# A fused attention-and-mixer kernel on one core: two token-weight blocks transposed on TensorE, cos and sin products joined, and the engine orders written anew

## The chip, the cores and the metric

The kernel runs on one core of a Trainium2 chip, in one launch. The metric is the device time in microseconds of that core; the kernel before takes 236.05 us, the median of 3 runs from 234.23 to 237.71. The profiled run took 235.77 us, of which the profile's span covers 233.9.

The engines are named as in the profile: PE is TensorE's matmul stream and PEld its weight loads, DVE is VectorE, ACT is ScalarE, POOL is GpSimd, and SP is the engine whose queue issues every DMA of this kernel.

## The reference

An attention stage feeds a mixer stage. There are 4 batches, 8 heads, 768 positions, head width 64; the mixer's width is 8 x 64 = 512.

```
# attention, per head; chunks of 32 keys, each query keeps 6 of 24
ub     = sum_d max(q * k_min(chunk), q * k_max(chunk))     # a bound for each query and chunk
sel    = the 6 chunks of highest ub that are not in the future
scores = q k^T / 8, masked to sel and to j <= i
attn   = softmax(scores);  x = attn v                      # heads side by side: x is (768, 512)

# mixer, per batch
theta  = x @ w_theta
y      = w_tok_r @ (x * cos(theta)) + w_tok_i @ (x * sin(theta))    # w_tok_* are 768 x 768
u      = x + y
out    = u + relu(u @ w_ch)
```

## The kernel before

**How it is written.** `record()` calls `op()` or `alt()` once for each piece of work: a name, an engine (with `alt`, a choice of engines), a planned duration in nanoseconds, what is read and written, and the function that emits the instructions. The n-th call is number n. The string `ORDER` (L17) then lists these numbers in the order in which they are emitted; a trailing `b` or `c` takes the second or third engine of an `alt`, and `F5` puts 5 small filler matmuls on PE. Each engine runs its own instructions strictly in this order, so `ORDER` fixes five queues. It also hands out buffers: `decode()` gives the next free one of a class at first use and takes it back after the last. The classes and their counts stand in `CLASSES` (L105 on): six landing buffers `ld` for everything that is loaded, three PSUM banks `mi` for most matmul results, two PSUM pairs `sc` for scores, one `av` for attention times v.

**Names used here**, with b for batch, p for a pair of heads, h for a head, t for one of six blocks of 128 positions:

- `Lq`, `Lk`, `Lv` load a pair's q, k, v (one transfer for each head of q and k). `Tq`, `Tk` transpose them on PE in two halves (three 128x128 fp32 transposes each). `evk`, `evq` evict the result from PSUM, `red0`, `red1` take the chunk maxima and minima on DVE, `kd` their difference, `cq` and `relu` derive the two forms of q.
- `ub.b.p` (L482) computes the bounds of two pairs on PE, 32 matmuls. Then a chain on DVE selects the chunks: `t1` (transpose), `cz`, `mx` (nine MAX8), `lt`, `t2`, twice; `cp` copies the masks into `qx`.
- `sc.b.h.s` (L554) are the scores, in three steps for a head, `ex` the exponentials on ACT (L560), `tri` the triangular mask, `av.b.h.i` (L401) the product with v, `norm` the division on DVE. Batch 0 uses a variant of these (L336 to L376).
- The mixer, `mixer(b)`: `Tx` and `evx` transpose x for batches 0 and 1 (batches 2 and 3 do it by DMA, `Dx`). `th.b.t` (L608) is theta, four matmuls of 512 columns; `sin` and `cos` follow on ACT (L615, L619), then the two products `zi = x*sin` and `zr = x*cos` (L623), one instruction each, on DVE or POOL. `mix.b.t.si` (L633, L635) are two 512-column matmuls; block t of y needs all six si. `u` adds x on DVE, `Tu` or `Du` transposes u, `ch` is the product with w_ch, `ot` the last sum on DVE, `out` the store.
- The weights: `Lwth`, `Lwch` and `Lwtok.ri.tt` load, `cwth`, `cwch`, `cwtok` cast to fp16. A token-weight block (ri 0 is real, 1 is imaginary, tt is one of six) must also be transposed: `Twtok.ri.tt` (L702) does this by a DMA from SP's queue. `mix.b.t` reads blocks (0, t) and (1, t).

The pieces of the code that the change touches most are the product and the token-weight transposes:

```
for nm, dst, src in (("zi", zi[t], sn), ("zr", zr[t], cs)):          # L624
    al = [("POOL", 1100, 1, ...), ("DVE", 342, 1, ...)]
    alt(f"{nm}.{b}.{t}", al if nm == "zi" else al[::-1], ...)
...
op("SP", f"Twtok.{ri}.{tt}", 1270, [(a, 0)], [("wtok", (ri, tt))], tr, dma=1200)   # L703
```

Of the kernel before, what the change touches and what calls it, by code (L numbers as in the profile page):

```python
# [10 lines left out]
FP32 = mybir.dt.float32  # L11
FP16 = mybir.dt.float16
ALU = mybir.AluOpType
# [5 lines left out]
    "3 1 4 31 2 29 28 30 0 21 58 17 57 14 18 729 15b F5 5 9 20b 55 730 7 16 10 56 477 11 F19 32 406 36 6 19 "  # L19
    "109 39 44 451 41 8 13b 34 48 12 23 37 75 45 38 42 33 47b 24 22b 40b 450 25 F12 50 35 83 26 68 27 71 51 82 "  # L20
    "69 176 72b 85 161 177 52 162 167 178 84 63 74 59 53 168 405 64 110 164 102 61 163 173 165 65 169 60 174 "
    "54 F9 170 67b 166b 113 77 43c 66 62b 46 171 175 196 78 49b 76 202 79 179 203 185 115 183 197 181 172b 193 "
    "125 80 204 81 90 194 198 190 92 184 91 191 195 199 186 95 200 192 187 96b 98 70b 73 93b 201 86 188 376 "
    "99b 213 103 140 87 211 375 101b 180 88 114 225 401 214 182 94b 210 402 116 104 377 89 189 134 226 126 378 "
    "209 105 228 127 227 216 212 229 205 230 217 222 106 403 207 215b 265 223 404 107 386 218 108 219 266b 389 "
    "224 381 387b 379 100 206 220 111 390 97 412 208 254 413 221 242 382 415 232 255 383b 243 231 256 248 384 "
    "135 233 388b 414 239 249 244 234 131 235 236 136 385 237 240 245 250 238 267 246 391 251 416 241 268 269 "
    "252 380 476 407 247 392 410 128 270b 259 253 411 258 257 393 112c 263 262 141b 260 137 261 394 408 264 "
    "142 395 417 409 132c 271 396b 418 397 133 272 420 419 129c 283 398b 130 421 138c 278 285 424 422 273 139 "
    "423 293 279 287 155 274 427 281b 121 295 146 276b 152 294 297 149 280 428 288 158 296b 275 437 298 429 "  # L30
# [12 lines left out]
    "503 775 747c 504b 507 583 757b 506c 505c 1067 774 601 776 785 598 584 602 820 777 613 786 778 821 593 603 "
    "599 569 787 591 592 570 610b 572 788 594 600 811 573 803 571b 595 779 807 812 798 575 596 574b 1069 780 "
    "822 1070 801 783c 805 606 789 597 576 614 802 784c 604 615 605 792c 826 887 577 607 800 890 616 824 817 "
    "806 823 579 580 799 578 825 793c 804 840 617 581 808b 619 891 781c 618 827 620 625 888 1092 892 906 626 "
    "1091 627 828 889 1071 628 907 893 1072b 629 829 1073b 894 1074 900 631 830 895 897 903 841 1075 898 831 "
    "896 639 1089 899 832b 630 634 633 641 632b 908b 640 644 643 635 642b 649 636 637b 646 638 654 645 648 651 "
    "666 647b 667 656 653b 668 655 669 1090b 657b 659 658 660 650 1135 661 790b 1134 652b 901 687 688 689 662 "
    "690 691 904 902 692 663 782b 905 693 791b 664 670 705 665 867 864 868 911 671 701 865 869b 880 672 909 "  # L50
    "910 881 809 866 702 912 835 810 882 833 836 877 815 834 813c 1113 861 878 839 719 1156 838 862 842 720 "
    "879 814 721 707 852 863 843 837 872 853 874 708 871 854 875 680 709 1114 870 1084 844 873 673 876 1180 "
    "1085 674 845 884 675 855 846 1076 856 681 1077 1159 847 858c 885 857b 1158 883 1078b 850c 682 851b 1079 "
    "1157 929 1080 945 930 683 848c 886 1093 1081b 684 1094 849c 946 685 931 926 859c 686 932 947 927 1095 "
    "860c 704 1100 1098 676 1102 928 1099 958 933 677 1101b 1137 1096 678 1103 1136 934 1097 919 1104 937 959 "
    "935 679 936 1105b 920 1082 960 938 1108 703 1083 1106 921 1109 916 1088 1087b 1086 955 1161 716 1107 1160 "
    "956 1112 710 1111 717 917 913 957 718 711 1110 1115 914 712 918 713 1116 915 1125 924 1117 923 1126 1118 "
    "922 1143 1181 942 1127 1145 939 1144 1119 694 943 1128 695 1120 696 1129 940 1122c 1146 952 1123c 697 925 "
    "1124c 1131b 698 953 941 1147 1130c 1227 714 1133c 699 1228 954 1233 715 700 1138 1121c 1151 1234 944b "
    "1230 706 1132 1141 1229 1152 949 1235 1231 1139b 1240 962 1142 1162 1241 1232 1246 1166 963 1148b 961 "  # L60
    "1164b 950 1247 1242 1243 964 1140 948 1248 1214 1244 951 1149 1173 1163b 1150 1236 968 1245 1220 1174b "
    "1215 1153 1237 1165 1238 1167 1239 1221 967 1154 1175 1204 1176 1169b 1222 1251 1250 1205 1171 1177 965 "
    "1207 1170 1249 722 1216 1208 1252 1172b 1206 970 1168 1217 1209 723 1201 1218 1179 986 724 1155 966 1178c "
    "1202 1182 1219 987 1203 969 1223 1192 1224 1225 1183 971 1226 988 996 989b 972 1184 990 1212 973 1185 "
    "1211 1210 998 981 974b 1186 997 1213 975b 976 982 1187 983 991 999b 978 1189 1188 985 1008 977 980 1256 "
    "992 1000 1253 979b 993 1022 994b 984b 1254 1009 995 1023 1193 1191c 1194 1015 1190c 1016 1195 1017 1196 "
    "1257 1024 1255 1018 1197c 1259 1199c 1010 1200c 1260 1011 1258 1012 1261 1013 1198 1279 1014 1025 1280 "
    "1026 1044 1262 1298 1281 1292 1299 1019 1293 1263 1300 1295 1264 1001 1296 1294 1265 1285 1027 1286 1297 "
    "1282 1028 1020 1287 1283 1269 1046 1021 1303 1301 1270 1302 1284 1266 1304 1045 1289 1267 1271 1272 1290 "
    "1288 1052 1273 1291 1268 1002 1274 1053 1276 1275 1277 1054 1029 1278 1030 1031 1305 1032 1055 1310 1003 "  # L70
    "1056 1004 1005 1309 1006 1036 1007 1037 1306 1038 1311 1307 1033 1312 1034 1039 1308 1035 1040 1041 1313 "
    "1314b 1331 1047 1042 1336 1315 1332 1057 1333 1043 1334b 1058 1337 1335 1316 1338 1339b 1048 1059 1326 "
    "1318 1340 1060 1317 1061 1320 1327 1319 1321 1328 1062 1329b 1376 1063 1322 1330 1362 1323 1324b 1363 "
    "1377 1325 1064 1378 1065 1379 1364 1066 1348 1349 1365 1350 1351 1352 1353 1380 1354 1366 1367 1384 1341 "
    "1368 1342 1343 1386 1049 1344 1050 1345 1346 1051 1355 1347 1356 1357 1383 1394 1358 1395 1359 1360 1396 "
    "1400 1361 1381 1385 1401 1369 1382 1370 1371 1402 1391 1372 1392 1373 1374 1393 1389 1375 1397 1390b 1387 "
    "1398 1406 1388b 1399 1403 1407 1408 1404 1405 "
)

B, H, S, D = 4, 8, 768, 64  # L80
P = 128
DM = H * D
NT = S // P
CH = 32
NCH = S // CH
QS = 192
NS = S - QS
# [3 lines left out]
NEG = -1000.0  # L91
KX = D + NCH
ROW = (0,)
X_DMA = (2, 3)
U_DMA = {(b, t) for b in (1, 2, 3) for t in range(NT) if b < 3 or t < 4}
SEGS = [(0, 4), (1, 3), (2, 5)]
BASE = [0, 1024, 2048]
# [61 lines left out]
def record(G):  # L159
# [417 lines left out]
    def mixer(b):  # L577
# [25 lines left out]
        for t in range(NT):  # L603
# [10 lines left out]
            def sin(ps=ps, sn=sn):  # L614
                nc.scalar.activation(out=T(sn), in_=T(ps), func=AF.Sin, bias=0.0, scale=1.0)  # L615
# [280 lines left out]
```

The softmax here doesn't subtract the row's maximum and nothing guards it: scores larger than these inputs give would overflow.

## Time and profile before

| stretch of the span | what runs in it | what the profile has there |
|---|---|---|
| 0 to 52 us | batch 0's attention, first weights, batch 1's first half | first `th` at 44.27, first `mix` at 51.67 |
| 52 to 88.3 us | batch 0's mixer, batch 1's first four heads | `ub.1.2` (batch 1's second half) starts at about 88.3 |
| 88.3 to 112.7 us | batch 1's last four heads, parts of batch 2 | `th.1.0` starts at 112.69 |
| 112.7 to 233.9 us | mixers of batches 1 to 3, the attention of 2 and 3 | last `ch` ends at 230.15 |

PE runs 2091 matmuls, DVE 517 instructions, ACT 248, POOL 196. The granted PE clock is full nearly throughout (mean 0.997). SP issues 170 DMAs: 64 loads of q and k, 16 of v, 20 of weights, 6 of small constants, 24 stores, and 40 transposes (12 `Twtok`, 12 `Dx`, 16 `Du`).

A reader of such a page should keep apart how long one matmul is shown (a 512-column one has a mean of 379 ns) and how often one can start: in the chain of waits four of them take 0.86 us, 0.216 us each, since they overlap. "Busy" on PE is therefore no measure of how much room is left.

### The profile page before, as it was taken

The numbers are of one execution on the slowest core, as the hardware profiler recorded it, in microseconds if no ns is written. First come the engines' busy times: TensorE is split into PE (matmuls) and PEld (weight loads), VectorE is DVE, ScalarE is ACT, GpSimd is POOL, SyncE is SP. The second block draws the span as 40 slices with busy tenths as digits, with TensorE's granted clock in tenths as the row PEclk, the third lists the DMA queues.
The fourth block names the chain that finished last, engine by engine and source line by source line (L and its number), as shares of the span: only waits on it lengthen the run. The fifth ranks groups of instructions, "written<-read, shape, count | busy, mean of one in ns | idle before, by whom it ended". The sixth has DMA issues, their size and how long they took to land.

```text
span 233.9 us, 5656 instructions
## 1 busy us (share of the span) xinstructions
PE 217.7 (93%) x2091; PEld 125.2 (53%) x2091; DVE 171.0 (73%) x517; ACT 165.2 (71%) x248; POOL 98.0 (42%) x196
## 2 busy tenths in 40 slices
PE   6999999898899997788999999999999999999993
PEld 2766566633446664456544666557654564444441
DVE  2699789797827999999963798699988263662353
ACT  2589989993938556999998759789999690550011
POOL 8645855335253222657311656765742440010000
PEclk9999999999999999999999999999999999999998
DMA  7999989989999999943614597602630135541443
GB/s 164 246 265 211 272 214 269 238 209 276 275 288 233 285 284 254 278 111 83 147 44 90 122 270 174 182 7 65 93 92 0 22 48 121 135 128 55 102 156 136
DMA packets 106526, 38.84 MB, mean 166 GB/s; under 512 B 100620, under 2 KB 100748, under 8 KB 106500
## 3 DMA queue, kind: packets, MB, share of 16 engines
q1 hardware_dynamic: 106500, 38.50, 68.6%
q8 instruction: 16, 0.26, 0.5%
q14 instruction: 10, 0.08, 0.1%
HBM read 26.17 MB, written 6.29 MB: 139 GB/s over the span
## 4 chain that ended last, share of the span: by engine, by line
PE 69%; DVE 12%; DMA 7%; ACT 5%; issue 2%; POOL 2%; SPq 2%; POOLq 0%; ACTq 0%; DVEq 0%
PE y L633 11%; PE y L635 11%; PE ch L662 9%; PE sc L554 8%; PE av L401 7%; PE th L608 7%; DMA wtok<-in_moe_w_tok_r_dram 5%; DVE km L445 3%; PE qps L433 3%; PE ub L482 2%; PE sc L341 2%; ACT kx L169 2%; PE kps L433 2%; DMA k<-in_k_dram 2%; PE ub L277 1%
## 5 line engine op out<-in xcount | busy, mean ns | idle before, releaser
L560 ACT ACTIVATE pt<-sc 128x1024 f16<-128x1024 f32 (+1 forms) x72 | 62.6, 920 | 9.9 <-PE sc L554 9.4
L633 PE MATMUL y<-zr,wtokT 128*128 128x512 f16 x144 | 54.6, 379 | 0.0
L635 PE MATMUL y<-zi,wtokT 128*128 128x512 f16 x144 | 54.5, 379 | 0.0
L554 PE MATMUL sc<-qx,kx 88*128 88x512 f16 (+3 forms) x192 | 37.1, 305 | 5.9 <-ACT pt L560 2.9
L570 POOL TENSOR_SCALAR_AFFINE_SELECT pt<-pt 128x256 f16<-128x256 f16 x60 | 24.1, 407 | 32.5 <-ACT pt L560 31.4
L401 PEld LDWEIGHTS <-pt 128*128 128x128 f16 x672 | 26.9, 98 | 9.2 <-issue 2.3
L401 PE MATMUL av<-v,pt 128*128 128x65 f16 x672 | 30.6, 194 | 1.3 <-POOL pt L570 0.4
L641 DVE TENSOR_TENSOR u<-y,x 128x512 f16<-128x512 f32 x24 | 16.4, 688 | 15.9 <-PE y L635 15.9
L554 PEld LDWEIGHTS <-kx 88*128 88x128 f16 x192 | 16.7, 97 | 21.2 <-issue 3.4
L668 DVE SCALAR_TENSOR_TENSOR ot<-ch,u 128x512 f32<-128x512 f32 x24 | 16.5, 688 | 13.7 <-PE ch L662 13.5
L445 DVE TENSOR_REDUCE km<-kps 128x12 f32<-128x384 f32 x48 | 24.9, 547 | 1.9 <-PE kps L433 1.3
L172 POOL CAST qx<-qT 64x768 f16<-64x768 f32 (+1 forms) x25 | 19.9, 797 | 14.4 <-ACT qT L169 12.4
L169 ACT CAST kx<-kps 64x384 f16<-64x384 f32 (+1 forms) x39 | 17.9, 475 | 10.9 <-PE kps L433 8.3
L662 PE MATMUL ch<-wch,uT 128*128 128x512 f16 x96 | 24.3, 379 | 0.1
L608 PE MATMUL th<-wtheta,xT 128*128 128x512 f16 x96 | 22.6, 379 | 0.6 <-ACT sn L615 0.6
L633 PEld LDWEIGHTS <-wtokT 128*128 128x128 f16 x144 | 14.0, 97 | 14.6 <-issue 0.3
L357 ACT ACTIVATE pt<-sc 128x1024 f16<-128x1024 f32 (+1 forms) x24 | 21.1, 922 | 0.9 <-PE sc L349 0.7
L635 PEld LDWEIGHTS <-wtokT 128*128 128x128 f16 x144 | 14.1, 98 | 14.0 <-issue 0.6
L615 ACT ACTIVATE sn<-th 128x512 f16<-128x512 f32 x24 | 14.0, 618 | 8.7 <-PE th L608 8.6
L412 DVE TENSOR_TENSOR x<-av,rec 128x384 f16<-128x384 f32 x32 | 17.8, 557 | 1.1
L526 POOL COPY qx<-nsT 24x288 f16<-24x288 f16 x29 | 12.6, 436 | 12.2 <-DVE nsT L518 11.0
L619 ACT ACTIVATE cs<-th,pi 128x512 f16<-128x512 f32 x24 | 16.3, 708 | 0.4 <-PE th L608 0.4
(95 smaller groups left out, 334.1 us busy)
## 6 DMA issues: line engine op xcount, KB each, us to landing
q<-in_q_dram SPq DMA_DIRECT2D x32, 192.0 KB, 3.3
k<-in_k_dram SPq DMA_DIRECT2D x32, 192.0 KB, 3.4
v<-in_v_dram SPq DMA_DIRECT2D x16, 384.0 KB, 4.4
out_dram<-ot SPq DMA_DIRECT2D x24, 256.0 KB, 2.0
wtok<-in_moe_w_tok_r_dram SPq DMA_DIRECT2D x6, 384.0 KB, 5.5
wtok<-in_moe_w_tok_i_dram SPq DMA_DIRECT2D x6, 384.0 KB, 5.6
wth<-in_moe_w_theta_dram SPq DMA_DIRECT2D x4, 256.0 KB, 4.1
wch<-in_moe_w_ch_dram SPq DMA_DIRECT2D x4, 256.0 KB, 4.2
```

The lines of the kernel that those rows point to most:

```text
L169: c = {"A": ("ACT", int(n * 0.833 + 60), 0, lambda: nc.scalar.copy(out=out(), in_=in_())), "D": ("DVE", int(n / 0.96 + 70) if psum else in ...
L172: "P": ("POOL", int(n * 0.833 + 140), 1, lambda: nc.gpsimd.tensor_copy(out=out(), in_=in_()))}
L357: nc.scalar.activation(out=T(pt)[:, :, base:base + w], in_=T(ps).rearrange("p (x c) -> p x c", x=2)[:, :, 0:w], func=AF.Exp, bias=0.0, sca ...
L401: nc.tensor.matmul(ps[:, t, :], T(pt)[:, x, o:o + P], T(v16)[:, x, j, :], start=(j == 0), stop=(j == t))
L445: nc.vector.tensor_reduce(out=T(km)[:, j, 12 * f:12 * f + 12], in_=T(ps)[:, 0:384].rearrange("p (c w) -> p c w", w=CH), axis=AX.X, op=o)
L554: nc.tensor.matmul(T(ps)[:, a0:a1], T(kx)[0:KX, x, j * P:(j + 1) * P], T(qx)[0:KX, x, q0 + a0 - o:q0 + a1 - o], start=True, stop=True)
L560: nc.scalar.activation(out=T(pt)[:, x, BASE[s]:BASE[s] + w], in_=T(ps)[:, 0:w], func=AF.Exp, bias=0.0, scale=SCALE)
L570: eng.affine_select(out=a, in_=a, pattern=[[0, 2], [1, P]], compare_op=ALU.is_ge, fill=G.zero_reg(), base=0, channel_multiplier=-1)
L608: nc.tensor.matmul(T(ps), T(xT[t])[:, c, :] if by_dma else T(xT[c])[:, t * P:(t + 1) * P], K.wtheta[:, c, :], start=(c == 0), stop=(c == 3))
L633: nc.tensor.matmul(T(ps), K.wtok[:, si, 0, t * P:(t + 1) * P], T(zr[si]), start=(si == 0), stop=False)
L635: nc.tensor.matmul(T(ps), K.wtok[:, si, 1, t * P:(t + 1) * P], T(zi[si]), start=False, stop=(si == NT - 1))
L662: nc.tensor.matmul(T(ps), T(uT[t])[:, c * P:(c + 1) * P], K.wch[:, c, :], start=(c == 0), stop=(c == 3))
```

## The change

It has five parts.

1. **Token weights.** A new constant `W_DMA = (2, 3, 4, 5)`: blocks tt = 0 and 1, real and imaginary, are no longer transposed by DMA but on PE (`Tw`, six 128x128 fp16 transposes into a PSUM bank) and evicted by DVE or ACT (`evw`). In the new order three `evw` are on ACT and one is on DVE.
2. **Joined products.** `sin` and `cos` write the two halves of one tile `cs`, and one instruction of 1024 elements for each block makes both products, with x read twice through a broadcast. It runs on DVE for 23 of the 24 blocks and on POOL for one. Before, 43 of the 48 products were on DVE and 5 on POOL.
3. **More choices of engine.** `relu` may run on POOL (4 of 16 do, 8 are on ACT, 4 on DVE; before, 9 on DVE and 7 on ACT); `cz` may run on POOL (8 of the 12 of batches 1 to 3 do; before all were on DVE). Of the 12 `cwtok` casts 10 are on POOL now (before 3, with 5 on DVE and 4 on ACT). Of the 32 `cq` copies 11 are on DVE (before 4).
4. **The end.** For `LAST = (3, 4)`, `ch`, `ot` and `out` are done in two halves of 256 columns.
5. **The orders.** All of `ORDER` is new, and with it all five queues. `qT` has four buffers in place of three. `K_SB` is empty, so the branches that ask for it do nothing.

The PE queue around the part that the title of the change names reads as follows, translated from the numbers (commas join steps or blocks of the same thing, `...` leaves out).

```
before:
 ... Tx.0.3 Tq.1.1.0,1 th.0.2,1,0,4 ub.1.0 th.0.3,5 mix.0.1.0,1 mix.0.0.0 ... sc.1.2.0 ... mix.0.4.0,1,2,3 mix.0.5.0,1 sc.1.3.0,2
 mix.0.5.2,3,4 ch.0.0 ... Tq.1.2.1 av.1.2.1 ... ch.0.5 Tk.1.2.0,1 ... mix.0.3.0,1,2,3 av.1.1.2,1,0 mix.0.3.4,5 ch.0.4 Tq.1.3.0 Tk.1.3.1
 ... Tq.1.3.1 Tu.0.3 ch.0.1 Tq.2.0.1 ch.0.3 ub.1.2 Tq.2.0.0 Tx.1.1 Tq.2.1.0,1 Tk.2.0.1,0 sc.1.5.2,1 Tk.2.1.1,0 sc.1.7.0,1 sc.1.5.0
 ub.2.0 ... av.1.7.0,2,1 Tk.2.3.1 Tx.1.2 sc.2.3.2 Tx.1.3 Tk.3.0.0 sc.2.2.2 th.1.0 ...
after:
 ... Tw.1.0 Tx.0.2 av.0.6.2 av.0.7.2 Tw.0.1 av.0.6.1 av.0.7.1,0 Tw.1.1 av.0.6.0 Tq.1.0.0,1 Tq.1.1.1 Tx.0.3 Tq.1.1.0 Tk.1.1.0
 th.0.0,1,3 ub.1.0 th.0.2,5,4 mix.0.2.0,1,2 mix.0.0.0,1 ... mix.0.3.0,1,2,3,4,5 ... Tk.1.3.1,0 ... mix.0.5.0,1,2,3,4,5 Tq.1.3.0,1
 sc.1.1.1 ch.0.3 Tu.0.5 sc.1.0.2 sc.1.2.0 av.1.3.1 ub.1.2 ch.0.5 av.1.0.0,2 Tq.2.0.0,1 mix.0.4.0,1,2,3,4,5 Tq.2.1.1 av.1.0.1
 Tk.2.0.1 Tu.0.4 Tq.2.1.0 sc.1.5.2 av.1.2.0,2,1 ch.0.4 ... ub.2.0 ... sc.2.2.1,0 av.2.3.2 Tx.1.3 ... av.2.3.0 th.1.1,0 ...
```

SP's queue from the loads of batch 1 on, in the same way:

```
before:
 ... Lwth.2 Lwth.3 Lwtok.0.0 Lk.1.0.1 Lwtok.1.2 Lk.1.0.0 Lk.1.1.0 Lk.1.1.1 Lq.1.0.0 Lwtok.1.1 Lq.1.0.1 Twtok.0.0 Lq.1.1.0
 Lq.1.1.1 Loh.1.0 Lwth.1 Lwtok.0.1 Twtok.1.1 Loh.1.3 Lwtok.1.0 Lwtok.0.2 Twtok.1.2 Twtok.0.1 Twtok.1.0 Twtok.0.2 Lwtok.0.5 Lwch.2
 Lwtok.1.3 Lwtok.1.4 Lwtok.0.4 Lwtok.1.5 Twtok.0.5 Lwch.3 Lwch.0 Twtok.1.4 Twtok.0.4 Twtok.1.5 Lwch.1 Lwtok.0.3 Lv.1.0 Lv.1.1
 Lq.1.2.1 Lq.1.2.0 Twtok.1.3 Lk.1.2.1 Lk.1.2.0 Lk.1.3.0 Lk.1.3.1 Twtok.0.3 Lv.1.2 Lq.1.3.0 Lq.1.3.1 out.0.2 ...
after:
 ... Lk.1.0.0 Lk.1.0.1 Lwth.3 Lwtok.0.0 Lwth.2 Lwtok.0.2 Lwth.0 Lwtok.1.2 Lk.1.1.1 Lk.1.1.0 Lwtok.1.0 Lwtok.0.1 Twtok.0.2 Lq.1.0.1
 Lwtok.1.1 Lq.1.0.0 Lq.1.1.1 Lq.1.1.0 Loh.1.0 Twtok.1.2 Lwth.1 Lwtok.0.4 Loh.1.3 Lwtok.0.5 Lwtok.1.3 Lwch.3 Lwch.0 Lwtok.1.5
 Lwtok.0.3 Twtok.0.4 Twtok.0.5 Lwtok.1.4 Lwch.1 Twtok.1.3 Lwch.2 Lv.1.0 Lq.1.2.0 Lq.1.2.1 Lk.1.2.0 Lk.1.2.1 Twtok.0.3 Twtok.1.4
 Lv.1.1 Lv.1.2 Lk.1.3.1 Lk.1.3.0 Twtok.1.5 Lq.1.3.0 out.0.2 Lq.1.3.1 ...
```

The core of the diff (the strings of `ORDER` are left out):

```diff
 ORDER = (
...
+K_SB = set()
+LAST = (3, 4)
+W_DMA = (2, 3, 4, 5)
...
-    "qT": (3, (S,), FP32, "sb", False),
+    "qT": (4, (S,), FP32, "sb", False),
...
-    "cs": (3, (DM,), FP16, "sb", False),
-    "sn": (3, (DM,), FP16, "sb", False),
-    "zr": (10, (DM,), FP16, "sb", False),
-    "zi": (10, (DM,), FP16, "sb", False),
+    "cs": (3, (2, DM), FP16, "sb", False),
+    "z": (10, (2, DM), FP16, "sb", False),
...
+                              ("POOL", 640, 1, lambda: relu(nc.gpsimd))],
...
+            alt(f"cz.{gn}.{x}", [("DVE", 145, 0, lambda cz=cz: cz(nc.vector)), ("POOL", 210, 1, lambda cz=cz: cz(nc.gpsimd))],
+                [], [(ubT, 0)])
...
-            def fz(eng, dst, src, t=t):
-                eng.tensor_tensor(out=T(dst), in0=T(x16)[:, t, :], in1=T(src), op=ALU.mult)
...
+            def fz(eng, dst=z[t], src=cs, t=t):
+                eng.tensor_tensor(out=T(dst), in0=T(x16)[:, t, :].unsqueeze(1).broadcast_to([P, 2, DM]), in1=T(src), op=ALU.mult)
+            alt(f"zr.{b}.{t}", [("DVE", 610, 1, lambda fz=fz: fz(nc.vector)), ("POOL", 2300, 1, lambda fz=fz: fz(nc.gpsimd))],
+                [(cs, 0), (cs, 1)] + xh, [(z[t], 0)])
...
+            parts = ((0, DM, ""),) if (b, t) != LAST else ((0, DM // 2, ""), (DM // 2, DM, "h"))
...
-                def tr(ri=ri, tt=tt, a=a):
-                    nc.sync.dma_start_transpose(out=K.wtok[:, :, ri, tt * P:(tt + 1) * P], in_=T(a))
-                op("SP", f"Twtok.{ri}.{tt}", 1270, [(a, 0)], [("wtok", (ri, tt))], tr, dma=1200)
+                if tt in W_DMA:
+                    op("SP", f"Twtok.{ri}.{tt}", 1270, [(a, 0)], [("wtok", (ri, tt))],
+                       lambda a=a, wt=wt: nc.sync.dma_start_transpose(out=wt(), in_=T(a)), dma=1200)
+                    continue
+                ps = buf("mi", f"wps.{ri}.{tt}", (S,), FP16)
...
+                    for c in range(NT):
+                        nc.tensor.transpose(T(ps)[:, c * P:(c + 1) * P], T(a)[:, c * P:(c + 1) * P], K.ident16)
+                op("PE", f"Tw.{ri}.{tt}", 330, [(a, 0)], [(ps, 0)], tr)
+                alt(f"evw.{ri}.{tt}",
+                    [("DVE", 470, 0, lambda ps=ps, wt=wt: nc.vector.tensor_copy(out=wt(), in_=T(ps).rearrange("p (c t) -> p c t", t=P))),
+                     ("ACT", 705, 0, lambda ps=ps, wt=wt: nc.scalar.copy(out=wt(), in_=T(ps).rearrange("p (c t) -> p c t", t=P)))],
+                    [(ps, 0)], [("wtok", (ri, tt))])
```

What it is for: with four transposes fewer in the DMA queue the loads behind them can move up; with `mix.0.4`, which needs late token weights, behind `ub.1.2`, the selection of batch 1's second half can begin while there is still mixer work of batch 0 for PE; and one product in place of two saves an instruction for each block.

## The prediction

> **What bounds the kernel now.** I read the busy shares first, then the busy time by stage, then the chain of waits in the two stages where PE has gaps, then the rows of the operations that the change touches.
>
> ```profile
> PE 217.7 (93%) x2091; PEld 125.2 (53%) x2091; DVE 171.0 (73%) x517; ACT 165.2 (71%) x248; POOL 98.0 (42%) x196
> ```
>
> PE looks full, but this is time in which some matmul is under way. I need the time that the queue of PE asks for. The planned durations in the code are start-to-start times: a `ch` is planned at 864 ns, and the chain of waits has "PE ch L662 x4" at 0.86 us. Summed over PE's queue they give 200.6 us. The last `ch` ends at 230.15 us, so PE loses 29.6 us before it; behind it stand 3.8 us for the last sum and store. I follow this loss as a lag: the time at which an operation starts less the PE work queued ahead of it. From the timeline: 13.2 us at the first `th` (44.27 less 31.1), 14.4 at the first `mix` (51.67 less 37.2), 18.4 at `ub.1.2` (88.3 less 69.9), 26.9 at `th.1.0` (112.69 less 85.8), 29.6 at the end. So the loss arises before 113 us, and PE is nearly dense after it. The busy time by stage says who holds it up:
>
> ```profile
> core 0: us, PE busy (x) PEld busy (x) DVE busy (x) ACT busy (x) POOL busy (x), PEclk, DMA share, GB/s
> 0.00:52.00 52.00, 47.44 (x605) 29.71 (x606) 40.98 (x132) 42.83 (x66) 29.65 (x67) 1.00 0.99 232
> 52.00:88.30 36.30, 34.02 (x274) 19.15 (x272) 27.97 (x78) 22.39 (x34) 13.79 (x21) 1.00 1.11 271
> 88.30:112.70 24.40, 19.42 (x249) 12.75 (x249) 23.08 (x90) 22.03 (x36) 13.81 (x28) 1.00 0.79 186
> 112.70:234.00 121.30, 116.85 (x972) 63.55 (x970) 78.94 (x221) 77.92 (x116) 40.74 (x81) 0.99 0.42 102
> ```
>
> From 52 to 88 us DVE and ACT idle (8.3 and 13.9 us) and the DMA engines are full: work waits for data. From 88.3 to 112.7 us DVE works 23.08 of 24.40 us and ACT 22.03: what could not be done earlier is now due at once, and PE waits for it. The chain in these stages:
>
> ```profile
> 50.93 7.01 DMA wtok<-in_moe_w_tok_r_dram
> ...
> 58.04 0.83 ACT wtok L169
> ```
>
> ```profile
> 95.81 1.85 DVE km L445 x4
> 97.66 0.29 DVE ns L513
> ...
> 101.68 1.55 DVE t L509 x18
> ...
> 112.69 0.90 PE th L608 x4
> ```
>
> The first piece shows a token weight that lands 7 us after its issue, with its cast and the PE queue behind it; the second the reductions and selections of several pairs in a row on DVE.
>
> **What the Trainium skill says.** "Perfetto Trace Analysis", Identifying the Most-Contended Engine, holds that matmul occupancy is no good measure on PE while occupancy is fair for DVE and ACT; the trace agrees (a 512-column matmul is shown at 379 ns and starts every 216). The same page, Optimization Strategy, advises interleaving regimes that have different bottlenecks; that is what moving `ub.1.2` ahead of `mix.0.4` does. "VectorE: DVE Perf Modes", in its perf-mode tier table, gives a 16-bit `tensor_tensor` in SBUF two elements a cycle, at 0.96 GHz; the trace agrees, 437 and 416 ns for 512 elements, of which that rate explains 267. "SBUF — State Buffer", Who interferes with whom, says that a DVE instruction with two SBUF inputs contends with GpSimd's reads; no row here separates that.
>
> **The change part by part.**
>
> *Joined products.*
>
> ```profile
> L623 DVE TENSOR_TENSOR zr<-x,cs 128x512 f16<-128x512 f16 x22 | 9.4, 437 | 1.2 <-ACT cs L619 1.0
> L623 DVE TENSOR_TENSOR zi<-x,sn 128x512 f16<-128x512 f16 x21 | 8.6, 416 | 2.6 <-ACT sn L615 2.1
> L623 POOL TENSOR_TENSOR zi<-x,sn 128x512 f16<-128x512 f16 x3 | 3.6, 1216 | 18.0 <-ACT sn L615 18.0
> ```
>
> The fixed part of one is 437 - 267 = 170 ns, so 1024 elements take 533 + 170 = 703 ns if the broadcast keeps the rate, 1067 + 170 = 1240 if it halves it. I take 703: 23 x 0.70 = 16.2 us on DVE in place of 18.0, and POOL loses 6.4 and gains one of about 2.4. At 1240 ns DVE would have 10 us more. The product now waits for sin and cos both; behind it on DVE stand `t1`, `mx`, `lt`, and `mix` waits for it. ACT needs 1.07 us for a pair as planned (480 and 588 ns; its rows show 618 and 708, which overlap), longer than PE's 0.864 for a `th`, so the wait is for ACT, as before.
>
> *Token weights on PE.* Adds 4 x 0.33 us of PE (a `Tx` is the same six transposes) and four evictions, rows of 551 ns on DVE and 809 on ACT for the same shape: 0.6 us of DVE, 2.4 of ACT. Takes four transposes out of SP's queue:
>
> ```profile
> L702 SPq DMA_TRANSPOSE wtokT<-wtok x12: 1211/1230/1354, 33.7 to 71.0; - x12
> ```
>
> They move 0.2 MB each, 0.73 us at 271 GB/s, and SP issues one in 1.23 us; the cost of one in a full queue lies between, and I take the upper, as transposes issued one after another leave the DMA engines short. Four make 4.9 us.
>
> *The new DMA order* pulls both ways. Counting bytes in the two queues, `Lwth.1` has 1.38 MB more ahead of it: at the first stage's 232 GB/s it comes 5.9 us later. It is issued at 37.1 us and lands 4.1 us on (median of its row), 41.2, so now at about 47; with a cast of 0.6 the first `th` moves from 44.3 to 47.4. Behind the waiting `th` stand `ub.1.0` and everything of PE. The later loads come earlier: `Lq.1.3.1`, the last of batch 1, issued at 74.3 and landing at about 77.6, has 0.52 MB less and four transposes less ahead: about 4 us earlier. The same count for every `Tk`, `Tq` and `Twtok` of the new queue asks for a lag of 13.8 us at most (before: up to 15 at `mix.0.4.0` and 17 at `Tk.2.2`).
>
> *PE's new order.* First `mix`: six `th` (5.2 us) and `ub.1.0` (1.2) after 47.4 make 54.0, less 38.7 of work queued ahead: lag 15.3, nearly as before (14.4), so the four `Tw` cost nothing; they stand where PE waits for weights anyway. From there to `ub.1.2` PE is given 25.4 us of work; with data in time I allow 0.7 us for short waits: lag 16, so `ub.1.2` starts at 64.1 + 16 = 80.1, not 88.3.
>
> Then DVE is the bound. In the old order DVE has 22.4 us planned between `ub.1.2` and `th.1.0`, and took 24.4: 2.0 over. In the new one it has 27.7 between `ub.1.2` and `th.1.1` (the first of the new order), against 25.4 on PE. So `th.1.1` starts at 80.1 + 27.7 + 2.0 = 109.8, with 89.5 us of PE work done: lag 20.3 against 26.9.
>
> From there PE is the bound again: 202.1 in all (200.6, plus 1.3 of `Tw` and three fillers) less 89.5 leaves 112.6. I add the 2.7 us of lag that the old order gathered in this part: the last `ch` ends at 225.1.
>
> *The end.* The last `ot` has 256 columns: 691 ns fall to about 425 (half of 533 less), and half the bytes to store; I take 0.5 us off 3.8. The span is 228.4; the profiled run took 1.9 us more than its span, and its time is 0.3 below the median: 230.5.
>
> *`relu` and `cz` on POOL, `cq` on DVE*: about -2, -0.9 and +3.3 us of DVE, already in the 27.7. POOL has 42% busy to take them; but ten `cwtok` casts now stand in its queue, each waiting for its load, with `tri` and `cp` behind. `cp.1.0.1` stands behind `cwtok.1.4`, whose load I put at about 59; `sc.1.1.0`, which needs that mask, is due at about 62. Just enough, so nothing. `qT`'s fourth buffer costs nothing.
>
> **The rivals.**
>
> *The gain is eaten on the way (28%).* For it: the first `th` comes late by construction, and DVE has more work in its full stretch than before. If the loads slip as much as before up to `ub.1.2` (lag 18.4, 82.5) and DVE runs 4% over plan (1.1 us), `th.1.1` is at 113.3 and the time 234.0. Against it: the count of bytes.
>
> *It is slower than before (7%).* The broadcast halves the rate: 6 x 0.54 = 3.2 us in batch 0's mixer, the same again for batch 1's, where `mix.1` waits for it, and POOL's casts hold the masks for three loads of 1.4 us (0.39 MB at 271 GB/s): 230.5 + 3.2 + 3.2 + 4.2 = 241. Against it: the triangular product at L568, two-dimensional and 16-bit, takes 343 ns for 256 elements, 133 of them at the double rate.
>
> *More is gained (13%).* DVE idles 8.3 us between 52 and 88; if it uses 3.5 of these for reductions whose loads now come early, the full stretch shrinks by as much: 227.
>
> **How the numbers follow.** The forecast has 52%: 230.5. The range 226.5 to 235.5 takes in the gain above and most of the eaten gain and leaves out the slower case. A gain of 2% is 231.3, and the forecast lies only 0.8 under it, with some 2 us to either side from the sizes that I chose: two thirds of it (0.35), all of the larger gain (0.13) and a little of the eaten gain (0.04) make 0.52 for faster. Slower by over 2%, above 240.8, takes most of that rival, 0.06. The rest, 0.42, is within 2%.
>
> **What would show it.** Right: `ub.1.2` near 80, the first `th` near 47, the joined product near 700 ns, DVE above 90% from 80 to 110 us, `th.1.1` near 110, and the last `ch` some 115 us after it. Wrong: a first `th` after 50, products above 1 us, a PE gap of several us before `mix.0.3` or `mix.0.5` (late transposes), or a stretch after 115 us in which PE waits for DVE or ACT.

## The result, and the profile after

The kernel after takes 228.69 us (median of 4 runs, 227.81 to 229.46) beside 235.66 us for the kernel before in the same comparison: a ratio of 0.970, 95% interval 0.961 to 0.978. The forecast was 230.5 in a range of 226.5 to 235.5, with "faster" the likeliest outcome; the measured time is 1.8 us below the forecast. A second comparison of the same kernel, `after_again` below, gave 228.58 us and the ratio 0.970 (0.962 to 0.978).

The page of the kernel after begins its busy shares so:

```profile
PE 215.9 (95%) x2122; PEld 127.3 (56%) x2122; DVE 175.2 (77%) x505; ACT 164.9 (73%) x247; POOL 94.1 (41%) x190
```

PE is busy for less time than before (215.9 against 217.7 us) though it has 31 matmuls more, and DVE is busy for 4 us more: so the gain isn't less work. The busy time by stage shows where it came from. The stages run from the first `th` to the first `mix`, from there to `ub.1.2`, to the first `th` of batch 1, and to the end of the last `ch`; the columns are those of the same view in the prediction.

```profile
core 0: us, PE busy (x) PEld busy (x) DVE busy (x) ACT busy (x) POOL busy (x), PEclk, DMA share, GB/s
46.70:53.80 7.10, 6.58 (x59) 2.75 (x57) 6.62 (x19) 7.04 (x13) 5.54 (x9) 1.00 0.93 274
53.80:79.80 26.00, 25.92 (x174) 14.62 (x172) 22.10 (x51) 19.91 (x31) 11.15 (x22) 1.00 1.16 253
79.80:109.50 29.70, 27.33 (x381) 19.29 (x378) 27.78 (x96) 25.82 (x40) 21.92 (x46) 1.00 0.90 215
109.50:223.90 114.40, 113.73 (x948) 62.22 (x944) 80.91 (x217) 76.25 (x112) 29.63 (x60) 1.00 0.42 97
```

Read the first number after each window, its length, and then the two or three fullest engines. First `mix` to `ub.1.2` took 36.6 us before (51.7 to 88.3) and takes 26.0 now, and PE, which had 2.3 us without work there, has 0.08. The full stretch up to batch 1's first `th` took 24.4 us, with PE busy for 19.42, and takes 29.7 now, with PE busy for 27.33. So PE's work was moved into a stage where PE has idle time. By the planned durations PE's queue asked for 32.7 us in the first of these stages before and asks for 25.4 now: of the 10.6 us won there, 7.3 are work moved away and 3.3 are waits that are gone. In the second it asked for 15.9 us and asks for 25.4, which is 9.5 us more work for 5.3 us more time, so waits went there too. The rest of the program is 3.1 us shorter (114.4 against 117.5), the way from the first `th` to the first `mix` and the end 0.5 together, and the first `th` came 2.4 us later in this run.

Where the chain of waits before had a token weight that took 7 us to land, the chain after reads:

```profile
50.91 0.69 DVE z L632
51.60 0.76 DVE ubT L507 x2
52.36 0.73 DVE t L519 x9
53.09 1.23 DVE z L632
```

Start, duration, what: no transfer stands in it there any more. It runs from product to product on DVE, with the selection of batch 1's first half between them. And where it had four reductions in a row on DVE, it has this in the full stretch:

```profile
89.36 0.47 ACT kx L169
...
90.33 0.92 ACT pt L570
...
92.14 1.02 ACT pt L570
93.17 0.02 issue
93.19 0.47 ACT kx L169
...
94.17 0.94 ACT pt L570
```

These are exponentials and evictions on ACT, one behind the other. The chain goes through ACT from 89.4 to 95.1 us and from 99.2 to 105.1, some 11 of the 29.7 us; the rest, some 18 us, is PE's own work, and no piece of it is on DVE, which the prediction had named. PE's waits in this stretch (in total, times, longest):

```profile
PE sc L564 <- ACT pt L570: 1.0, 2, 0.5
PE av L402 <- ACT pt L570: 0.8, 1, 0.8
PE qps L434 <- ACT kx L169: 0.2, 1, 0.2
```

All end on ACT, and they are 2.0 of the 2.4 us in which PE has no matmul under way there. The rows of the operations in question:

```profile
L632 DVE TENSOR_TENSOR z<-x,cs 128x1024 f16<-128x1024 f16 x23 | 16.7, 743 | 5.7 <-ACT cs L628 2.9 <-ACT cs L624 2.6
L716 SPq DMA_TRANSPOSE wtokT<-wtok x8: 1220/1302/2097, 33.2 to 67.3; - x8
L195 POOL TENSOR_SCALAR qr<-qT 128x576 f32<-128x576 f32 x4 | 6.6, 1645 | 2.3 <-ACT qT L169 1.7 <-DVE qT L171 0.6
```

The joined product is 743 ns on average (shortest 677, median 692). The issue of a DMA transpose has a median of 1302 ns (shortest, median, longest in the middle column), much as before. `relu` on POOL takes 1645 ns, where 640 were planned.

### The profile page after: what moved, and what is told of

Same layout as the page of the kernel before. It is cut to its first block, busy times and chain, and to the rows that moved or that the text cites. A ratio compares the mean times of both kernels' runs of the same rounds, so it can differ in the third digit from the quotient of the medians.

```text
span 227.4 us, 5663 instructions
## 1 busy us (share of the span) xinstructions
PE 215.9 (95%) x2122; PEld 127.3 (56%) x2122; DVE 175.2 (77%) x505; ACT 164.9 (73%) x247; POOL 94.1 (41%) x190
## 4 chain that ended last, share of the span: by engine, by line
PE 64%; ACT 11%; DMA 8%; SPq 7%; DVE 5%; issue 2%; POOL 1%; DVEq 0%; ACTq 0%
PE y L640 13%; PE y L642 13%; PE sc L564 9%; PE ch L673 8%; PE av L402 6%; PE th L617 5%; DMA v<-in_v_dram 4%; SPq L179 4%; ACT pt L570 3%; SPq L600 2%; PE qps L434 2%; DMA wth<-in_moe_w_theta_dram 2%; PE kps L434 2%; PE ub L491 2%; ACT pt L358 2%; ACT kx L169 2%
## 5 line engine op out<-in xcount | busy, mean ns | idle before, releaser
L640 PE MATMUL y<-z,wtokT 128*128 128x512 f16 x144 | 54.6, 379 | 0.1
L642 PE MATMUL y<-z,wtokT 128*128 128x512 f16 x144 | 54.5, 379 | 0.0
L580 POOL TENSOR_SCALAR_AFFINE_SELECT pt<-pt 128x256 f16<-128x256 f16 x62 | 25.5, 415 | 49.0 <-ACT pt L570 47.6
L402 PEld LDWEIGHTS <-pt 128*128 128x128 f16 x672 | 27.7, 98 | 7.7 <-ACT pt L570 1.4
L673 PE MATMUL ch<-wch,uT 128*128 128x512 f16 (+1 forms) x96 | 23.6, 374 | 0.0
L678 DVE SCALAR_TENSOR_TENSOR ot<-ch,u 128x512 f32<-128x512 f32 (+1 forms) x24 | 16.3, 678 | 7.5 <-PE ch L673 7.3
L169 ACT COPY qT<-qps 128x384 f32<-128x384 f32 x24 | 11.2, 486 | 14.6 <-PE qps L231 7.7
L632 DVE TENSOR_TENSOR z<-x,cs 128x1024 f16<-128x1024 f16 x23 | 16.7, 743 | 5.7 <-ACT cs L628 2.9
L172 POOL CAST qx<-qT 64x768 f16<-64x768 f32 (+1 forms) x18 | 14.5, 811 | 12.2 <-ACT qT L169 7.5
L413 DVE TENSOR_TENSOR x<-av,rec 128x384 f16<-128x384 f32 x32 | 17.8, 557 | 1.1
L169 ACT CAST kx<-kps 64x384 f16<-64x384 f32 (+1 forms) x36 | 16.7, 477 | 2.3 <-PE kps L434 1.0
```

What stands on the lines that cost most here:

```text
L169: c = {"A": ("ACT", int(n * 0.833 + 60), 0, lambda: nc.scalar.copy(out=out(), in_=in_())), "D": ("DVE", int(n / 0.96 + 70) if psum else in ...
L402: nc.tensor.matmul(ps[:, t, :], T(pt)[:, x, o:o + P], T(v16)[:, x, j, :], start=(j == 0), stop=(j == t))
L413: nc.vector.tensor_tensor(out=T(x16)[:, :, h * D:(h + 1) * D], in0=ps[:, :, 0:D], in1=T(rec).broadcast_to([P, NT, D]), op=ALU.mult)
L580: eng.affine_select(out=a, in_=a, pattern=[[0, 2], [1, P]], compare_op=ALU.is_ge, fill=G.zero_reg(), base=0, channel_multiplier=-1)
L640: nc.tensor.matmul(T(ps), K.wtok[:, si, 0, t * P:(t + 1) * P], T(z[si])[:, 0], start=(si == 0), stop=False)
L642: nc.tensor.matmul(T(ps), K.wtok[:, si, 1, t * P:(t + 1) * P], T(z[si])[:, 1], start=False, stop=(si == NT - 1))
```

## The experiments

Twelve kernels, each timed beside the kernel before on the same chip. The first `th` starts between 44.6 and 47.2 us in the profiled runs of kernels whose work up to there is the same, so I compare the lengths of stages. Between the two profiles of the kernel after the first stage differs by 0.3 us; the full stretch, to hundredths, is 29.64 or 29.65 us in all five profiles in which no edit touches it:

| kernel | time, us | ratio to before (95%) | first `mix` to `ub.1.2` | `ub.1.2` to `th.1.1` |
|---|---|---|---|---|
| after | 228.69 | 0.970 (0.961 to 0.978) | 26.0 | 29.7 |
| after_again | 228.58 | 0.970 (0.962 to 0.978) | 25.8 | 29.6 |
| mix04_first | 231.94 | 0.984 (0.976 to 0.992) | 28.3 | 29.9 |
| tw_dma | 232.13 | 0.985 (0.978 to 0.992) | 29.8 | 29.6 |
| both_undone | 235.12 | 0.989 (0.981 to 0.996) | 31.6 | 30.0 |
| z_two | 228.32 | 0.968 (0.960 to 0.975) | 25.6 | 29.6 |
| relu_dve | 228.73 | 0.973 (0.967 to 0.979) | 26.1 | 30.0 |
| dve_load_b1 | 229.58 | 0.977 (0.970 to 0.984) | 26.0 | 30.0 |
| dve_load_b3 | 229.28 | 0.975 (0.970 to 0.981) | 26.0 | 29.7 |
| dve_less | 228.83 | 0.964 (0.957 to 0.971) | 26.0 | 29.7 |
| act_less | 227.74 | 0.960 (0.953 to 0.966) | 26.0 | 28.8 |
| both_less | 226.75 | 0.956 (0.949 to 0.962) | 26.1 | 28.2 |

both_undone and the three with `less` shared a chip on which the kernel before took 237.33 us, at a mean granted clock of 0.985 to 0.993 in all its runs, against 234.8 to 235.7 us for the others. dve_less has the stages and the time of the kernel after and yet a ratio of 0.964, so compare across the two groups by stage or by time, not by ratio. The twelfth, before_ub_early, stands at the end.

**after_again.** No edit.

> The changed kernel once more, unaltered, on the chip of the three runs beside it: 228 to 229.5 us, first theta at about 46.7 us, ub.1.2 at about 79.8, th.1.1 at about 109.5. All theories expect the same of it; it is what the others are compared with.

It repeats the result and its stages.

**mix04_first: the new place of `mix.0.4` undone.** Everything else as in the kernel after.

```diff
 (PE's queue, in names)
- ... av.1.3.1 ub.1.2 ch.0.5 av.1.0.0,2 Tq.2.0.0,1 mix.0.4.0,1,2,3,4,5 Tq.2.1.1 ...
+ ... av.1.3.1 mix.0.4.0,1,2,3,4,5 ub.1.2 ch.0.5 av.1.0.0,2 Tq.2.0.0,1 Tq.2.1.1 ...
 (u.0.4 on DVE goes with it)
```

> The changed kernel with one thing undone: the six mix.0.4 (2.6 us of PE) and their sum u.0.4 stand ahead of ub.1.2 again. Theory (from ub.1.2 to th.1.1 DVE is the bound, so the start of ub.1.2 sets th.1.1): ub.1.2 at 82.4, th.1.1 at about 112, time about 231.2. Rival (PE's total sets the time, the order of two pieces of work does not matter): th.1.1 stays at 109.5 and the time at 228.7.

It costs 3.3 us. The busy time of its two stages:

```profile
52.10:80.40 28.30, 28.27 (x186) 15.55 (x184) 22.18 (x51) 21.60 (x33) 16.13 (x25) 1.00 1.06 247
80.40:110.30 29.90, 25.80 (x364) 18.56 (x364) 27.82 (x95) 23.98 (x37) 20.46 (x43) 1.00 0.85 204
```

The twelve matmuls (2.6 us at 0.216 each) make the first stage 2.3 us longer, where PE is busy for 28.27 of 28.30 us. The second has 12 matmuls fewer than in the kernel after, and isn't shorter for it. What they leave there is a wait, which the kernel after does not have (PE's timeline; the bracket is the idle time ahead of the instruction and who ended it):

```profile
87.48 0.55 PE L434 MATMUL qps<-ident,q 128*128 128x128 f32 x3 [1.55 <-ACT qT L169]
```

The chain of waits leads from it back over copies and a `relu` on ACT to the selection on DVE right behind `ub.1.2`. So the same work costs nearly its full time in a stage where PE is full, and nothing where it fills a wait. This is the interleaving of regimes that the prediction named, measured. The expectation's reason, that DVE bounds the full stretch, isn't shown by this run: any wait of PE there would give the same.

**tw_dma: the four token-weight blocks back on the DMA queue.** The transposes take the places of `Tw` in the order, ahead of the later loads, and `evw` is gone.

```diff
-W_DMA = (2, 3, 4, 5)
+W_DMA = (0, 1, 2, 3, 4, 5)
 (ORDER: Tw.0.0, Tw.1.0, Tw.0.1, Tw.1.1 -> Twtok of the same block; evw.* left out)
```

> The changed kernel with the four token-weight transposes on DMA again, each at the place of the PE transpose in the order. Theory (the early loads queue behind them): Lq.1.3.1 lands some 5 us later than at 74.4, of which about 2 us are slack before Tq.1.3 needs it, so ub.1.2 comes 2.5 to 3 us later, and 1.3 us of PE work are saved: time 230 to 231.2. Rival (transposes by DMA lie beside other transfers and cost nothing): PE has 1.3 us less to do and the time is about 227.5.

It costs 3.5 us, and all of it arises in one place. Its chain of waits from 46 to 57 us, then PE's and DVE's timeline there and the busy time from 53 to 60:

```profile
45.87 4.25 DMA wtok<-in_moe_w_tok_r_dram
50.12 0.05 issue
50.17 0.82 POOL wtok L172
51.00 2.76 issue
...
53.77 0.61 POOL wch L172
54.38 0.12 POOL ubT L513
54.50 0.03 issue
54.53 0.82 DVE t L519 x9
55.35 0.60 DVE z L632
55.95 0.04 issue
56.00 0.55 PE y L640
```

```profile
53.77 0.61 POOL L172 CAST wch<-wch 128x512 f16<-128x512 f32 x1 [2.77 <-DMA wch<-in_moe_w_ch_dram]
...
54.53 0.82 DVE L519 MAX8 t<-ubT 128x8 f32<-128x16 f32 x9 [3.39 <-POOL ubT L513]
...
56.00 0.55 PE L640 MATMUL y<-z,wtokT 128*128 128x512 f16 x1 [2.37 <-DVE z L632]
```

```profile
53.00:60.00 7.00, 4.60 (x13) 1.70 (x13) 5.44 (x27) 4.56 (x7) 5.78 (x6) 0.76 1.11 300
```

This is one delay handed through four queues. Four transposes more stand ahead of a load of `w_ch` in SP's queue: it is issued at 48.60 us, against 44.33 in mix04_first, whose first `th` is within 0.1 us of this one's. Its cast waits 2.77 us for it on POOL. Behind the cast stands `cz`, a memset of 0.17 us; for that `mx` waits on DVE, 3.39 us; behind `mx` stands a product; for that PE waits 2.37 us. Then the clock falls: the window's granted clock (last column but two) is 0.76, and the matmuls behind the gap start every 0.43 us (56.33, 56.76, 57.19, 57.61 ...) until 59, in place of every 0.22. Seven of them at 0.21 more are 1.5 us; with the gap of 2.4 that is the 3.8 to 4.0 us by which this stage is longer. From 60 us to `ub.1.2` PE is busy without a break, so no other late load holds it up.

The Trainium skill, "TensorE: Matmul & The Clock Gate", Part 1: The HAM clock gate, states that the array runs at half its clock after an idle window of about 3.4 us, the window running freely, and for about 3.4 us after work begins again. The halved rate agrees with this trace, and so does its length, 3.3 us from 56.0 to 59.3; the gap that was enough here is shorter, 2.4 us. In the profile of both_undone a gap of 3.0 us at the same place left the clock at 1.00. So a gap of this size may or may not cost twice.

**both_undone: the two together.** The edits of mix04_first and tw_dma.

> Kernel after with two parts undone at once: the four token-weight blocks transposed by DMA again (as in tw_dma) and mix.0.4 with u.0.4 ahead of ub.1.2 (as in mix04_first). Alone they cost 3.5 and 3.3 us. If each takes away its own part of the path to ub.1.2, the two add up: 228.6 + 6.8 = 235.4, the time of before (235.7), ub.1.2 about 32 us after the first mix in place of 26. If they compete for the same slack (late transposes hide the work of mix.0.4), less is lost: about 233, ub.1.2 about 30 us after the first mix. Joined products, the split end and the rest of the orders stay as they are in both.

The losses nearly add up, as in the first of the two cases expected. By stages: 31.6 us to `ub.1.2`, 5.6 more than after, which are a PE gap of 3.0 us at the product and the 2.6 us of `mix.0.4`. By time: 235.12 us against 228.83 for dve_less, timed beside the same kernel before and with the stages of the kernel after, which is 6.3 us; the two alone cost 3.4 and 3.5 us beside after_again. Its profiled run, at a clock of 1.00, is the fastest of its four (233.21 us); the other three had a mean clock of 0.989 to 0.993 (tw_dma's four: 0.985 to 0.993), so a loss by the clock is likely in them too, though no profile of them shows where. Without it, by the spans of the two profiles (231.5 and 226.3 us), the loss is 5.2 us. So these two parts bring some 5 to 6 of the 7.0 us gained, and the rest of the orders the remainder. The cascade is the same, a little longer on DVE:

```profile
54.41 0.82 DVE L519 MAX8 t<-ubT 128x8 f32<-128x16 f32 x9 [3.92 <-POOL ubT L513]
```

**z_two: the products parted again.** The tile, the order and the places stay; each `z` is two instructions of 512 elements.

```diff
-                eng.tensor_tensor(out=T(dst), in0=T(x16)[:, t, :].unsqueeze(1).broadcast_to([P, 2, DM]), in1=T(src), op=ALU.mult)
+                for j in (1, 0):
+                    eng.tensor_tensor(out=T(dst)[:, j], in0=T(x16)[:, t, :], in1=T(src)[:, j], op=ALU.mult)
```

> The changed kernel with the joined product made by two instructions of 512 elements in the same place of the order. Theory (one joined product costs DVE as much as two single ones started back to back, 0.69 us either way): 228.7, no change beyond 0.3 us. Rival (joining is a main part of the gain): slower by 2 us or more, with the products of batches 0 and 1 ending later.

```profile
L633 DVE TENSOR_TENSOR z<-x,cs 128x512 f16<-128x512 f16 x46 | 17.9, 440 | 4.4 <-ACT cs L624 3.8 <-ACT cs L628 0.5
```

46 instructions of 440 ns in place of 23 of 743: 1.2 us of DVE more, and no change of the time. In this order, joining brings nothing that can be measured.

**relu_dve: the four `relu` of POOL on DVE.** Their suffix `c` is dropped in `ORDER`.

> The changed kernel with the four relu that stand on POOL put on DVE. On POOL they take 1.65 us each where 0.64 was planned. Theory (they are hidden on POOL, and two of them would now lie in DVE's full stretch): 0 to 0.8 us slower, 228.7 to 229.5. Rival (the slow relu on POOL delay ub.2.0 and the masks behind them): about 1 us faster, 227.7.

The time is the same, though POOL needs 1645 ns for one and DVE about 450. POOL's time was hidden. Two of the four fall into the full stretch and make it 0.4 us longer, with DVE now in its chain for 5.3 us; the time does not show it.

**dve_load_b1 and dve_load_b3: work added on DVE**, in the full stretch (batch 1) or, for comparison, in batch 3.

```diff
+            if b == 1 and h > 3:      # dve_load_b3: b == 3
+                nc.vector.memset(K.zero, 0.0)
             nc.vector.reciprocal(out=T(rec), in_=ps[:, :, D:D + 1])
```

> The changed kernel with 2.4 us of useless DVE work added where the theory has DVE as the bound: a 512-element memset of a constant tile ahead of each of the four divisions of batch 1's heads 4 to 7. Theory: th.1.1 about 2.4 us later, time about 231. Rival (DVE's load there is hidden behind PE or ACT): no change, 228.7.

> The same four memsets ahead of the divisions of batch 3's heads 4 to 7, where PE is dense and DVE about half busy. Theory (PE is the bound there): 228.7, at most 0.5 us more. Rival (DVE's total sets the time): about 231, as with the other placing.

The dose was too small to decide what bounds the stretch. A memset of zero over 512 fp16 elements ran as one of 256 words:

```profile
L413 DVE MEMSET zero<- x4: 272/272/272, 98.6 to 108.1; 128x256 uint32 x4
```

Four of them are 1.1 us where 2.4 were meant. In batch 1 they made the full stretch 0.4 us longer (30.01 against 29.64), in batch 3 not; the two times, 229.58 and 229.28 us, don't differ beyond the noise. So added work on DVE is felt there, at a third of its size, though no piece of that chain is on DVE; this does not make DVE the bound, and the next three take work away instead.

**dve_less, act_less, both_less: what bounds the full stretch.** In the first, batch 2's sixteen chunk reductions, all in that stretch, read 8 of 32 keys. In the second, twelve exponentials do only the first 512, 512 and 384 columns, and what reads them is turned to those columns. The third has both.

```diff
 (dve_less)
-    in_=src.rearrange("p (c w) -> p c w", w=CH), axis=AX.X, op=o)
+    in_=src.rearrange("p (c w) -> p c w", w=CH)[:, :, 0:8 if b == 2 else CH], axis=AX.X, op=o)
 (act_less)
-    def ex(s=s, w=wa + wb, ps=ps, x=x):
+    def ex(s=s, w=(512, 512, 384)[s] if b == 1 and h > 3 else wa + wb, ps=ps, x=x):
...
+                        if b == 1 and h > 3:
+                            s = part[j]
+                            o = BASE[s] + (2 * P if t > j else 0 if j == SEGS[s][0] else P)
```

> Kernel after with less for DVE between ub.1.2 and th.1.1: the 16 chunk reductions of batch 2 read 8 of 32 keys of each chunk, 96 elements in place of 384 (the other keys are left out of the maxima and minima). All 16 stand in that stretch. The 545 ns row has 400 ns for its 384 elements if one takes 1/0.96 ns, so each should fall to about 245 ns: 4.8 us less for DVE. If DVE bounds the stretch, as I predicted, it falls from 29.7 us to 27.5 or less, where the work of ACT (25.8 us busy) and PE (25.4 planned) would hold it, and the time to about 226.5. If ACT alone bounds it, as the chain of waits from 89 to 105 us suggests, it stays at 29.4 to 30.0 and the time at 228.6. If the two hand the work to each other in turn, it falls by 0.5 to 1.5 us.

> Kernel after with less for ACT in the same stretch: the 12 exponentials of batch 1's heads 4 to 7 do only the first 512, 512 and 384 of their 1024, 1024 and 640 columns, and the products with v and the triangular mask read columns from that part (the other scores are left out). By the planned slope (918 ns for 1024 columns, 598 for 640, so 0.833 ns a column) that takes 8 x 0.43 + 4 x 0.21 = 4.3 us from ACT, with nothing changed in the number or size of the PE, DVE and POOL instructions. If ACT bounds the stretch it falls from 29.7 us to about 27.5 or less and the time to about 226.5. If DVE alone does, it stays at 29.4 to 30.0 and the time at 228.6. If the two take turns, it falls by 0.5 to 1.5 us.

> Both reliefs in one kernel (the same parts left out as in dve_less and act_less). DVE alone: as short as dve_less. ACT alone: as short as act_less. In turns, or two nearly equal bounds of which the second takes over: shorter than either by 1 us or more, down to PE's 25.4 planned plus the overs of the before kernel's stretch, about 26.5 us; the time then about 225.5.

The doses came out as meant, 545 to 246 ns for a reduction and 1030 to 599 ns for a long exponential:

```profile
L451 DVE TENSOR_REDUCE km<-kps 128x12 f32<-128x96 f32 x16 | 3.5, 246 | 2.9 <-ACT kx L169 1.6 <-PE kps L434 1.2
```

```profile
L573 ACT ACTIVATE pt<-sc 128x512 f16<-128x512 f32 x8 | 4.6, 599 | 0.1
```

The stretch in each of the three, one answer each:

```profile
78.10:107.80 29.70, 27.32 (x380) 19.30 (x378) 23.68 (x96) 25.82 (x40) 21.93 (x46) 1.00 0.87 208
```

```profile
78.50:107.30 28.80, 27.71 (x380) 19.16 (x378) 27.50 (x96) 21.96 (x40) 22.02 (x46) 1.00 0.89 215
```

```profile
78.10:106.30 28.20, 27.34 (x379) 19.33 (x378) 23.73 (x96) 21.92 (x40) 21.42 (x45) 1.00 0.91 219
```

With 4.1 us less on DVE (27.78 to 23.68) the stretch is as long as before, 29.7 us, and its chain still goes through ACT. With 3.9 us less on ACT it is 0.9 us shorter, and the chain changes hands; these pieces stand where ACT's stood:

```profile
88.70 2.32 DVE km L454 x5
...
91.16 0.56 DVE x L416
91.71 0.47 DVE kx L171
```

With both it is 1.5 us shorter. PE is then busy for 27.34 of 28.20 us, and its own work is 18.5 us of the chain, against 17.8 of 29.7 in the kernel after; ACT still has 5.7 us of it and DVE 3.7. So in this order ACT sets the length, in two parts of the stretch, and DVE would set it 0.9 us lower. The most that such relief could bring was small from the start: PE has no matmul under way for only 2.4 us of the stretch (29.70 less 27.33), and 0.9 us of that is left with both. Whether PE itself comes next can't be said, as its busy time overstates what its queue asks for, 25.4 us by plan. The three times fall in the same order, 228.83, 227.74 and 226.75 us, but their intervals overlap; the lengths of the stretch are the evidence. None of the three theories fits alone: dve_less contradicts DVE, and act_less is too small for ACT alone and both_less too small for turns. No version that spares ACT and computes the same was tried.

**before_ub_early: one part alone, in the kernel before.** In the old order `mix.0.3`, `u.0.3` and what follows from them go behind `ub.1.2`, and two late transposes behind the last load of batch 1.

```diff
 (PE)
- ... mix.0.3.0,1,2,3 ... mix.0.3.4,5 ... Tu.0.3 ... ch.0.3 ub.1.2 ...
+ ... ub.1.2 ... mix.0.3.0,1,2,3,4,5 ... Tu.0.3 ... ch.0.3 ...
 (SP)
- ... Twtok.1.3 Lk.1.2.1 ... Lk.1.3.1 Twtok.0.3 Lv.1.2 Lq.1.3.0 Lq.1.3.1 ...
+ ... Lk.1.2.1 ... Lk.1.3.1 Lv.1.2 Lq.1.3.0 Lq.1.3.1 Twtok.1.3 Twtok.0.3 ...
```

> The kernel before with one thing of the change done to its order: mix.0.3 (which waits for the last token weights there) and what follows from it stand behind ub.1.2, and the two transposes of these weights behind the loads of batch 1. Nothing else of the change. Theory: ub.1.2 at about 84 in place of 88.3, th.1.0 at about 110 in place of 112.7, since 1.6 us of sums move into DVE's full stretch; time about 233. Rival (the order alone gives nothing, the gain is from DMA and DVE work saved): 235.7.

A miss: 239.12 us, ratio 1.015 (1.007 to 1.023), slower than the kernel before. `ub.1.2` came at 87.0, only 1.3 us earlier, for the next wait stood right behind the one removed; and the stretch from there to `th.1.0` took 29.1 us in place of 24.3. Some 3.7 us of PE's planned work had been moved into it, and PE's idle time there stayed what it was (5.1 against 5.0 us), so the moved work filled none of it. Of its chain of waits ahead of `ub.1.2`:

```profile
77.64 1.02 DVE km L445 x2
...
80.24 1.47 PE ch L662 x4
...
86.09 0.83 POOL qx L172
```

PE waits for DVE's reductions and a division up to 79.4 us; the `ch` behind it takes 1.47 us where 0.86 is usual, the granted clock having fallen (a mean of 0.55 from 80 to 83.5 us); and at the end `ub.1.2` waits for a copy on POOL. So this part alone, in the old order, brings nothing. That it needs its loads, reductions and copies moved with it, and so a new order of all queues, is my reading; no run adds them one by one.

## Why the prediction was right, and where it wasn't

**Right in size.** `ub.1.2` was put at 80.1 and came at 79.8 to 79.9. The first `th` was put at 47.4 and came at 46.68, the first `mix` at 54.0 and 53.77, `th.1.1` at 109.8 and 109.47, the last `ch` at 225.1 and 223.86, the span at 228.4 and 227.4. The step "with data in time I allow 0.7 us for short waits" holds: PE is busy for 25.92 of 26.00 us there. Both parts that this step rests on were undone alone and cost 3.3 and 3.5 us. The product, "I take 703", has a median of 692 ns, so the broadcast keeps the rate.

**Wrong in cause: "Then DVE is the bound."** The sum 27.7 + 2.0 = 29.7 is the measured length, but dve_less shows that DVE doesn't set it: 4.1 us less of DVE's work changed nothing. The step took the engine with the largest planned sum for the bound. What holds the stretch is ACT, with 2 us less work than DVE, in 11 us of the chain and in all of PE's listed waits; 3.9 us less of its work make the stretch 0.9 us shorter. So the hit of 29.7 us is luck. The "2.0 over" plan was taken from the old stretch, where 3.3 of the 4.5 us of PE's listed waits ended on ACT too; that may be why the number came out although the name was wrong. A reason why the engine with less work holds PE up would be that each exponential frees a PSUM pair and each eviction a bank, for which PE's next scores and transposes wait in order. This is read from the chain and the code and wasn't tried by itself.

**The first `th`: right number, other cause.** "At the first stage's 232 GB/s it comes 5.9 us later": `Lwth.1` landed at 44.26, 3.3 us later than before's 41.0. Its cast ended at 44.93, and PE, busy with transposes in its queue, came to the `th` 1.8 us after that. It was issued 4.0 us later (41.06 against 37.08) and landed 3.2 us on where I took 4.1: the count of bytes was too high by some 2 us in the issue, and why wasn't tested. `Lq.1.3.1` was issued 3.5 us earlier, where I had said about 4.

**"Four make 4.9 us", right in size, incomplete in path.** In tw_dma a load behind four more transposes was issued 4.3 us later. But what this cost was not a later `Lq` at the end of the queue; it was a cast on POOL, and the queue behind it. The prediction named this danger, "ten `cwtok` casts now stand in its queue, each waiting for its load, with `tri` and `cp` behind", and looked at `cp.1.0.1`. There the room was larger than it thought: behind the cast, POOL stood idle for 2.6 us until DVE had the mask. The tight place was `cz`, some nine microseconds earlier, behind a cast of `w_ch`. In the kernel after that cast waits 1.24 us, `cz` ends at 52.23 and `mx` starts at 52.36: just enough. In tw_dma `cz` comes 4.0 us later, counted from the first `th`, and that is too late.

**Smaller terms.** "I add the 2.7 us of lag": it was 1.8 (114.4 less 112.6). "I take 0.5 us off 3.8": the end takes 3.6, so 0.2 off; the last `ot` is 415 ns as forecast (425), but an issue of 0.54 us stands ahead of it. `relu` on POOL is 1645 ns, not the planned 640, and hidden.

**The rivals.** "The gain is eaten" needed loads that slip; none held PE between 54 and 80 us. "Slower" needed products of half the rate, against 692 ns, or POOL's casts holding something back: tw_dma shows the second to be real, but in the kernel after the casts come just in time. "More is gained" put the time at 227; it ends 1.7 us above that.

## What to carry to other kernels

Ask of each stage what a piece of work costs there: the same twelve matmuls cost 2.3 us where PE was full and nothing where they filled a wait of PE, while parting the joined products, 1.2 us of DVE, changed nothing anywhere. That a stretch has idle time on PE is not enough, as before_ub_early shows: the moved work must stand where PE waits. The largest sum of planned durations doesn't name the bound; take work from one engine, then from another, then from both, and see which moves the end and what comes next. And on an in-order queue look behind each instruction that waits for a transfer: a memset of 0.17 us behind a late cast held up two other engines.

## What the runs showed of the hardware

Two instructions of DVE that ran beside a cast on POOL took 1.8 and 2.5 times as long as others of their kind. In the kernel after the product at 53.09 us took 1.23 us, where the median is 0.69, and `relu` on DVE took 1.13 us with casts on POOL at the same time, where it takes 0.44 to 0.46 in relu_dve. DVE's timeline and POOL's:

```profile
30.89 1.13 DVE L195 TENSOR_SCALAR qr<-qT 128x576 f32<-128x576 f32 x1
53.01 1.90 DVE L632 TENSOR_TENSOR z<-x,cs 128x1024 f16<-128x1024 f16 x2
```

```profile
30.88 0.82 POOL L172 CAST wtok<-wtok 128x768 f16<-128x768 f32 x1
...
52.16 1.59 POOL L172 CAST wtok<-wtok 128x768 f16<-128x768 f32 x2
```

The Trainium skill, "SBUF — State Buffer", Who interferes with whom, describes both cases: two inputs in SBUF, and a `tensor_scalar` in a mode that takes a second port, with the later one blocked until the other has ended. The trace agrees with that; the prediction had found no row for it. The granted clock of PE fell behind a pause of 2.4 us in tw_dma (matmuls at half the rate) and behind one of 1.7 us in before_ub_early (a mean of 0.55 over 3.5 us); it did not behind one of 3.0 us in the profile of both_undone.
